# Prologue of a Fourier-mixing and MoE kernel: zero matmuls at the start, moved S1 and S2 groups, filter copies as DMAs, a split first load

## Chip, cores, metric

One core of one Trainium2 chip. The metric is the time of one launch in microseconds; a run's time is its profiled span plus about 1.8 us. Times are medians of 4 to 11 runs. Ratios come from fast runs of the same job, and are not quite the ratio of the medians quoted beside them; the brackets after them are 95% intervals.

## The reference

```python
X = np.fft.rfft(x, axis=1)                    # x: (8, 3008, 256)
Y = X * (filt_r + 1j * filt_i)[None, :, :]    # filters: (1505, 256)
y = np.fft.irfft(Y, n=3008, axis=1)
h = y.reshape(24064, 256) @ w_in              # (256, 2048)
g = np.maximum(0.01 * h, h)
out = g @ w_out                               # (2048, 256)
```

## The kernel before

The transform over 3008 = 94 x 32 points is done as matmuls: S1 (over 94), a VectorE transpose T1, S2 (over 32), a multiply with the filters, SA, a second transpose T2, SB. Then come the two MoE matmuls. For batch 0 this is the prologue, done in two halves of 128 columns (`hf`) called half 0 and half 1, or first and second half, so that work can start before all of x is there; for later batches it is woven into the MoE. The filters (`fa_sb`, `fb_sb`) are loaded into partitions 0 to 63 and copied to partitions 64 to 127 by `upper`. "On pool" groups are multiplied by GpSimd after ScalarE has copied them out of PSUM, the memory that matmuls write to (`fx`, in buffers tagged p1 and p2); the others are multiplied by VectorE.

```python
    scrp = ctx.enter_context(tc.tile_pool(name="scr", bufs=2))
    ...
    def x_load(b, n0=0, nn=N2, d0=0, dn=D):
        for lo, cnt in ((0, R1),) if b + 1 < B else ((0, 64), (64, N1 - 64)):
            nc.gpsimd.dma_start(x_sb[lo : lo + cnt, ds(n0, nn), ds(d0, dn)], ...)
    ...
    for hf in range(2):
        for n0 in (0, N2 // 2):
            x_load(0, n0, N2 // 2, hf * DH, DH)
        filt_load(fa_sb, filt_r, hf * DH, DH)
        filt_load(fb_sb, filt_i, hf * DH, DH)
    nc.gpsimd.dma_start(i1_sb[:], i1_d.ap())
    nc.gpsimd.dma_start(w_in_sb[:], moe_w_in...)
    ...
    def first_s2(hf, c, n, on_pool):
        ps = bank("ph", n, DH)
        src = paired(big[1])              # "p (e n t) -> p n e t", t = 2
        for j in range(0, n, 4):
            nc.tensor.matmul(ps[...], fwd2, src[:, ds(c + j, 4), ts(hf, DH // 2)], ...)
        ...
        if on_pool:
            xs = [scrp.tile([P, 4, DH], FP32, tag=f"p{j // 4 + 1}", ...) for j in range(0, n, 4)]
            for j, xf in enumerate(xs):
                act(xf[:], ps[:, ts(j, 4), :])
            ...                           # nc.gpsimd.tensor_tensor with fa, then fb
        else:
            ...                           # nc.vector.tensor_tensor with fa, then fb
    ...
    def upper(hf):
        for t, cp in ((fa_sb, act), (fb_sb, dve)):
            cp(t[64:P, :, ts(hf, DH)], t[0:64, :, ts(hf, DH)])
    ...
    for g in range(8):
        first_s1(0, g, two[(g // 2) % 2], (act, dve)[g % 2])
    t1_part(0, 0, True)(), t1_part(0, 1, True)()
    upper(0)
    first_s2(0, 8, 8, True)
    first_s2(0, 0, 8, False)
    first_s2(0, 20, 4, True)
    first_s2(0, 16, 4, False)
    for g in range(8):
        first_s1(1, g, two[g % 4 == 3], dve if g in (3, 5, 7) else act)
    x_load(1)
    t1_part(0, 2, True)(), t1_part(0, 3, True)()
    upper(1)
    first_sa(0, 0), first_sa(0, 16)
    first_s2(1, 8, 8, True)
    first_s2(1, 0, 8, False)
    ...                                   # cut here; the rest is in the diff below
```

## Time and profile before

| | before |
|---|---|
| time, median of 5 | 785.42 us (784.65 to 787.25) |
| TensorE busy | 97% of the span |
| second x quarter used by S1 | 12.45 us |
| first VectorE multiply of half 1 | 31.29 us |
| first MoE matmul | 45.56 us |

The prediction below shows the slices and the timeline lines that carry the argument. Timeline lines read: start, duration, engine, source line, operation, output and inputs, count, and in brackets the engine's idle time before and what ended it. Two more lines of the kernel before:

```profile
20.47 0.59 ACT L268 COPY fx_h_c<-ph 128x512 f32<-128x512 f32 x1 [0.68 <-PE ph L260]
31.29 1.23 DVE L276 TENSOR_TENSOR fy_h_c<-ph,fa_sb 128x1024 f16<-128x1024 f32 x1 [1.04 <-ACT fx_h_c L268]
```

ScalarE's copy for the third GpSimd group waits for its matmul, and VectorE's first half-1 multiply for ScalarE's copy of the S2 output. The profiled run took 787.67 us, more than any of the five timed ones. The "granted clock" below is the share of TensorE's full clock that the profile says the throttle allowed.

### The profile page before, as it was taken

How to read it: one execution, taken by the hardware profiler on the slowest of the kernel's cores; microseconds unless marked ns; L12 is line 12 of the kernel's file. 1: busy time of each engine (PE TensorE's matmuls, PEld its weight loads, DVE VectorE, ACT ScalarE, POOL GpSimd, SP SyncE). 2: the span in 40 equal slices, each digit the busy share in tenths (PEclk: the TensorE clock that was granted, in tenths of full speed). 3: DMA queues.
4: the chain of work that ended last, by engine and by line, in shares of the span. 5: the costliest groups of instructions: out<-in, count | busy, mean ns of one | idle time of the engine just before them, and what ended most of it. 6: DMA issues, size and time to landing. Idle time of an engine off the chain costs nothing.

```text
span 785.9 us, 13623 instructions
## 1 busy us (share of the span) xinstructions
PE 763.0 (97%) x5812; PEld 528.6 (67%) x5812; DVE 365.1 (46%) x459; ACT 557.0 (71%) x794; POOL 150.7 (19%) x122
## 2 busy tenths in 40 slices
PE   2799999999999999999999999999999999999998
PEld 1356677666776677866777667776677667676666
DVE  3869760784327652387316754078432765200000
ACT  3686768676687767877687775967668776666664
POOL 5773400240003400052001410024000340000000
PEclk9999999999999999999999999999999999999999
DMA  9943010501032010501014101050100101101111
GB/s 174 214 59 94 28 42 28 122 28 41 28 79 70 28 41 28 119 31 41 28 41 108 41 28 41 28 120 28 42 28 28 41 28 42 41 28 41 41 41 54
DMA packets 42013, 43.39 MB, mean 55 GB/s; under 512 B 14274, under 2 KB 40514, under 8 KB 41282
## 3 DMA queue, kind: packets, MB, share of 16 engines
q0 software_dynamic: 15760, 16.99, 13.2%
q1 hardware_dynamic: 26192, 25.53, 9.3%
q8 instruction: 45, 0.74, 0.4%
q14 instruction: 16, 0.13, 0.1%
HBM read 34.10 MB, written 24.64 MB: 75 GB/s over the span
## 4 chain that ended last, share of the span: by engine, by line
PE 93%; ACT 2%; issue 1%; DVE 0%; ACTq 0%; DVEq 0%
PE po_ps L379 41%; PE ph L365 40%; PE pf L170 3%; PE pf L237 2%; PE pf L210 2%; PE pf L225 2%; PE pf L379 1%; ACT big L181 1%; ACT gt_c L370 1%; PE pf L284 1%; PE ph L260 0%; PE ph L301 0%; DVE fy_h_c L276 0%; PE po_ps L313 0%; PE pf L301 0%
## 5 line engine op out<-in xcount | busy, mean ns | idle before, releaser
L370 ACT ACTIVATE gt_c<-ph 128x1024 f16<-128x1024 f32 x376 | 384.8, 1024 | 194.8 <-PE ph L365 193.8
L365 PE MATMUL ph<-yt,w_in_sb 128*128 128x512 f16 (+7 forms) x1728 | 386.6, 351 | 0.4 <-ACT yt L304 0.2
L379 PE MATMUL po_ps<-w_out_sb,gt_c 128*128 128x256 f16 x2944 | 381.5, 272 | 0.6 <-ACT ost_c_t L386 0.6
L379 PEld LDWEIGHTS <-gt_c 128*128 128x128 f16 x3008 | 290.7, 98 | 86.7 <-issue 1.7
L365 PEld LDWEIGHTS <-w_in_sb 128*128 128x128 f16 x1728 | 163.0, 98 | 95.2 <-issue 1.0
L218 POOL TENSOR_TENSOR y_b_g<-p_b_g,p_b_g 128x512 f16<-128x512 f32 x84 | 106.9, 1273 | 225.5 <-DVE p_b_g L216 225.5
L181 ACT CAST big<-pf 128x512 f16<-128x512 f32 x195 | 111.8, 606 | 11.8 <-PE pf L251 11.7
L193 DVE STREAM_TRANSPOSE big<-big 128x1024 f32<-128x1024 f32 x32 | 55.8, 1846 | 127.1 <-ACT big L181 126.7
L240 DVE CAST yt<-pf 128x376 f16<-128x376 f32 x112 | 56.3, 545 | 85.9 <-PE pf L237 85.9
L214 DVE TENSOR_TENSOR p_b_g<-pf,fa_sb 128x512 f32<-128x512 f32 x84 | 58.1, 692 | 38.0 <-PE pf L210 35.5
L386 ACT COPY ost_c_t<-po_ps 128x256 f32<-128x256 f32 x184 | 69.4, 377 | 6.7 <-PE po_ps L379 5.6
L201 DVE STREAM_TRANSPOSE big<-big 128x1024 f32<-128x1024 f32 x28 | 51.1, 1936 | 34.5 <-ACT big L181 34.5
L215 DVE TENSOR_TENSOR p_b_g<-pf,fb_sb 64x512 f32<-64x512 f32 x84 | 58.2, 693 | 1.1
L216 DVE TENSOR_TENSOR p_b_g<-pf,fb_sb 64x512 f32<-64x512 f32 x84 | 57.4, 683 | 1.1
L132 POOL DMA_DIRECT2D x_sb<-in_x_dram x12 | 8.5, 713 | 256.6 <-PE pf L170 255.5
L237 PEld LDWEIGHTS <-big 128*128 128x128 f16 x448 | 25.7, 98 | 13.2
L170 PE MATMUL pf<-x_sb,f_sb 94*128 94x256 f16 x224 | 33.8, 272 | 0.1
L210 PE MATMUL pf<-big,small_sb 128*128 128x512 f16 x84 | 31.8, 379 | 0.0
L225 PE MATMUL pf<-y_b_g,small_sb 128*128 128x512 f16 x84 | 31.8, 379 | 0.0
L237 PE MATMUL pf<-i_sb,big 128*128 128x94 f16 x448 | 28.7, 206 | 0.0
L170 PEld LDWEIGHTS <-f_sb 94*128 94x128 f16 x224 | 21.0, 97 | 9.5 <-issue 1.3
L347 POOL TENSOR_SCALAR fb_sb<-fb_sb 64x6144 f16<-64x6144 f16 x1 | 15.7, 15742 | 0.4 <-DVE fy_h_c L276 0.4
(45 smaller groups left out, 142.8 us busy)
## 6 DMA issues: line engine op xcount, KB each, us to landing
out_dram<-ost_c_t SPq DMA_DIRECT2D x92, 256.0 KB, 2.1
x_sb<-in_x_dram POOLq DMA_DIRECT2D x6, 1536.0 KB, 11.3
x_sb<-in_x_dram POOLq DMA_DIRECT2D x4, 384.0 KB, 11.0
w_in_sb<-in_moe_w_in_dram POOLq DMA_DIRECT2D x1, 1024.0 KB, 14.9
w_out_sb<-in_moe_w_out_dram POOLq DMA_DIRECT2D x1, 1024.0 KB, 10.2
x_sb<-in_x_dram POOLq DMA_DIRECT2D x1, 1024.0 KB, 9.1
f_sb<-fwd_const SPq DMA_DIRECT2D x4, 192.0 KB, 3.2
fa_sb<-in_filt_r_dram POOLq DMA_DIRECT2D x4, 192.0 KB, 9.8
```

What stands on the lines that cost most here:

```text
L170: nc.tensor.matmul(ps[:, j, :], f1_sb[:N1, n2, :], x_sb[:N1, n2, :], start=True, stop=True)
L181: copy(paired(dst)[:, ds(n0, nn), ds(e0, de)], ps.rearrange("p n (e t) -> p n e t", t=2))
L214: nc.vector.tensor_tensor(p1[:], ps, fa, AL.mult)
L215: nc.vector.tensor_tensor(p2[0:64], ps[64:P], fb[64:P], AL.mult)
L216: nc.vector.tensor_tensor(p2[64:P], ps[0:64], fb[0:64], AL.mult)
L218: nc.gpsimd.tensor_tensor(y1[:], p1[:], p2[:], AL.add)
L237: nc.tensor.matmul(ps[:, j, :], src[:, dt, n2, :], i1_sb[:, n2, :], start=True, stop=True)
L240: copy(yv[:, :, ds(4 * h, 4)], ps.rearrange("p c a -> p a c"))
L365: nc.tensor.matmul(ph[:, j, ds(o, ln)], w_in_sb[:, dt, ts(ct, P)], yts[b % 2][:, dt, ds(lo, ln)], start=(dt == 0), stop=(dt == NDT - 1),)
L370: nc.scalar.activation(gts[ci][:, ds(2 * g, 2), :], ph, AF.Lrelu)
L379: nc.tensor.matmul(po, gts[ci][:, ct, ts(tj, P)], w_out_sb[:, ct, :], start=(ct == 0), stop=(ct == NCT - 1))
L386: nc.scalar.copy(ost[:, tj % 2, :], po)
```

## The change

The intent: warm the TensorE clock while x is on its way, fill TensorE's wait for a PSUM buffer with S1 groups of the second half, take the second half's filter copies off ScalarE and VectorE, let VectorE's last multiplies run on, and start the first x load with a smaller piece. The diff is cut at "..."; it also moves a memset of `big[2]` behind that of the zero tile.

```diff
-    def x_load(b, n0=0, nn=N2, d0=0, dn=D):
+    def x_load(b, n0=0, nn=N2, d0=0, dn=D, parts=None):
...
-            x_load(0, n0, N2 // 2, hf * DH, DH)
+            x_load(0, n0, N2 // 2, hf * DH, DH, None if hf else ((0, 64), (64, 32)))
...
     def upper(hf):
-        for t, cp in ((fa_sb, act), (fb_sb, dve)):
+        for t, cp in ((fa_sb, nc.sync.dma_start if hf else act), (fb_sb, nc.sync.dma_start if hf else dve)):
...
+    idle = scrp.tile([P, CH], FP16, tag="p1", name="idle")
+    nc.vector.memset(idle[:], 0.0)
+    keep_warm(24)          # now 128x128 by 128x512 matmuls of the idle tile into po_ps
...
     first_s2(0, 20, 4, True)
-    first_s2(0, 16, 4, False)
+    upper(1)
     for g in range(8):
+        if g == 3:
+            first_s2(0, 16, 4, False)
         first_s1(1, g, two[g % 4 == 3], dve if g in (3, 5, 7) else act)
     x_load(1)
     t1_part(0, 2, True)(), t1_part(0, 3, True)()
-    upper(1)
     first_sa(0, 0), first_sa(0, 16)
     first_s2(1, 8, 8, True)
     first_s2(1, 0, 8, False)
     nc.gpsimd.dma_start(w_out_sb[:], moe_w_out.rearrange("(ct p) d -> p ct d", p=P))
+    first_s2(1, 16, 8, False)
     first_sa(0, 8), first_sa(0, 20)
-    first_s2(1, 16, 8, False)
     first_sa(1, 0)
...
-    keep_warm(3)
     for g in range(8, 16):
```

More of the change, by code (lines that the diff above doesn't have):

```diff
@@ L127 @@
     DH = D // 2
-    def x_load(b, n0=0, nn=N2, d0=0, dn=D):
-        for lo, cnt in ((0, R1),) if b + 1 < B else ((0, 64), (64, N1 - 64)):
+    def x_load(b, n0=0, nn=N2, d0=0, dn=D, parts=None):
+        if b + 1 < B:
+            parts = parts or ((0, R1),)
+        for lo, cnt in parts or ((0, 64), (64, N1 - 64)):
             nc.gpsimd.dma_start(
@@ L160 @@
     nc.scalar.activation(one[:], one[:], AF.Lrelu)
-    nc.vector.memset(big[2][:].rearrange("p (e n t) -> p e n t", n=Q, t=2)[:, :, NC:Q, :], 0.0)
     def s1_group(b, g, copy=nc.scalar.copy):
@@ L312, in keep_warm @@
         for _ in range(n):
-            nc.tensor.matmul(po_ps.rearrange("p a d -> p (a d)"), small_sb[:, 0, :],
-                             i1_sb[:].rearrange("p a d -> p (a d)")[:, 0:512],
+            nc.tensor.matmul(po_ps[:].rearrange("p a d -> p (a d)"), idle[:, 0:P], idle[:],
                              start=True, stop=True)
+    idle = scrp.tile([P, CH], FP16, tag="p1", name="idle")
+    nc.vector.memset(idle[:], 0.0)
+    keep_warm(24)
+    nc.vector.memset(big[2][:].rearrange("p (e n t) -> p e n t", n=Q, t=2)[:, :, NC:Q, :], 0.0)
     for g in range(8):
```

## The prediction

> **What bounds the kernel now.** I read the page first: engine shares, slices, chain, groups. Then I read the first 60 us in time order, engine by engine, because every edited line is there.
>
> ```profile
> PE 763.0 (97%) x5812; PEld 528.6 (67%) x5812; DVE 365.1 (46%) x459; ACT 557.0 (71%) x794; POOL 150.7 (19%) x122
> ...
> PE   2799999999999999999999999999999999999998
> ```
>
> TensorE is busy for 97% of the span; of 40 slices (19.6 us each) only the first two are not full. From about 46 us on, the MoE matmuls set the pace, and the diff touches none of them. So the whole effect is how much earlier the first MoE matmul can start. Split in stretches, TensorE is busy 54.0 of the 54.4 us from 45.6 to 100 us, and 499.45 of the 500 us from 200 to 700 us: a microsecond won before the MoE should reach the end nearly undiminished, and nothing more can be won.
>
> ```profile
> 9.59 1.01 PE L251 MATMUL pf<-x_sb,f_sb 94*128 94x128 f16 x8 [9.59 <-DMA x_sb<-in_x_dram]
> 12.45 1.01 PE L251 MATMUL pf<-x_sb,f_sb 94*128 94x128 f16 x8 [0.99 <-DMA x_sb<-in_x_dram]
> 17.67 1.88 PE L260 MATMUL ph<-big,small_sb 128*128 128x512 f16 x4 [3.35 <-DVE big L193]
> 22.05 0.59 PE L260 MATMUL ph<-big,small_sb 128*128 128x512 f16 x1 [1.61 <-DVE fy_h_c L276]
> 29.31 1.88 PE L260 MATMUL ph<-big,small_sb 128*128 128x512 f16 x4 [1.33 <-DVE big L193]
> 45.56 1.28 PE L365 MATMUL ph<-yt,w_in_sb 128*128 128x512 f16 x4 [0.17 <-ACT yt L304]
> ```
>
> These timeline lines (start, duration, idle before) show TensorE waiting: for the first x quarter until 9.59 us, for the second until 12.45, for the first half's transposes until 17.67, for a PSUM buffer until 22.05, for the second half's transposes until 29.31. MoE starts at 45.56. The prologue is a relay of DMA, TensorE, ScalarE/VectorE evictions and VectorE transposes, bound by no engine's throughput.
>
> ```profile
> 26.29 2.75 ACT L308 COPY fa_sb<-fa_sb 64x3072 f16<-64x3072 f16 x1
> 26.88 2.37 DVE L193 STREAM_TRANSPOSE big<-big 128x1024 f32<-128x1024 f32 x2
> 29.29 0.96 DVE L308 COPY fb_sb<-fb_sb 64x3072 f16<-64x3072 f16 x1
> 34.70 1.22 DVE L276 TENSOR_TENSOR fy_h_c<-ph,fa_sb 128x1024 f16<-128x1024 f32 x1 [1.06 <-PE ph L260]
> 36.97 2.36 DVE L292 STREAM_TRANSPOSE big<-big 128x1024 f32<-128x1024 f32 x2
> 39.69 2.37 DVE L292 STREAM_TRANSPOSE big<-big 128x1024 f32<-128x1024 f32 x2 [0.35 <-ACT big L285]
> ```
>
> The reader is to see the two filter copies that become DMAs, the 1.06 us that VectorE waits for the last S2 group, and the last transposes.
>
> **What the Trainium skill says.** (1) "TensorE: Matmul & The Clock Gate", Part 1: the array starts at half clock and is released after about 3.4 us of activity in a free-running window. The trace agrees in kind: 128x512 S2 matmuls at 29.3 to 34 us last about 600 to 630 ns and start 0.43 us apart; from 34.4 us on the same shape lasts 376 to 390 ns. The granted-clock column reads 0.50 from 31 to 34 us and 1.00 afterwards, but also 1.00 before 29 us, where durations are slow; early on I trust durations. (2) The same page puts the return to half clock after about 3.4 us of idleness. The trace doesn't fit: at 27.6 us matmuls last 379 ns, TensorE then idles 1.33 us, and at 29.31 they last 600 again. I take warmth to survive about a microsecond, not three. (3) "DMA: Bandwidth & Descriptors", Rules for kernel authors: two transfers to disjoint partition parts share the same 16 engines and gain nothing. So splitting one load into 64 and 32 rows can gain only by an earlier start. The trace shows the software queue slow at first: 20 packets from 2 to 4 us, 496 from 4 to 6, then 1201, and a steady 1433 per 2 us.
>
> **The change part by part.**
>
> *24 zero matmuls at the start.* They need only a small memset, so they start near 1.2 us. Cold spacing is 0.43 us; half that, 0.216, follows from the five warm-keeping matmuls before (1.24 us for five, the last one's latency included). In this trace the array warmed 5.1 us after work resumed at 22.05 (27.2) and 4.7 after 29.31 (34.0). So I take about 5 us cold, 12 matmuls, then 12 at 0.216 = 2.6 us: the end is near 8.8 us, before x at 9.59. Cost on the path: none. Gain: S1's 128x128 matmuls run warm. Cold, a group of four takes 0.43 us (evictions start at 13.07, 13.58, 13.93, 14.36 and end at 15.05). Warm, TensorE outruns the evictions, two engines at 0.59 and 0.69 us: first group ready 0.45 us after the second x quarter, VectorE's first 0.3 later, two of 0.69 behind it: 12.45+0.45+0.3+1.38 = 14.58, against 15.05, **0.47 us**. The gap between the x quarters (about 1.6 us if warm) may lose the clock again; I count 0.3. The 3.3 us transpose wait at 14.3 to 17.7 almost surely loses it, so S2 stays cold.
>
> *The x load split.* The first part needs fewer descriptors built before it can start, but issues cost 0.6 to 1.1 us each on GpSimd and engines are saturated from 7 us on. I count **0.2**.
>
> *S1 groups 0 to 2 ahead of the (0,16) S2 group.* Now TensorE stands 1.61 us before 22.05 with all second-half S1 behind it. Afterwards three groups (12 x 0.107 = 1.3 us) fill that hole; their x landed by about 18.3 us (issued 6.26, some 12 us to land). The buffer still comes free at 22.00, so VectorE's multiplies still run 22.68 to 23.96. Groups 3, 5, 7 are then ready in time, and VectorE follows on without gaps: 23.96 + 3 x 0.65 = 25.9, against 26.78 before. Transposes start at 25.95 instead of 26.88: **0.93 us**.
>
> *upper(1) as two DMAs.* This takes 2.75 us from ScalarE and 0.96 from VectorE. VectorE's copy lay beside TensorE's S2 (VectorE waited 1.04 us after it): worth nothing. ScalarE's made the SA evictions wait until 29.06, but those are needed only by the transposes of 36.97. The DMAs (1536 pieces per tensor, at most 717 packets per us when alone, about half when shared) start after the filters land, 22 and 24.7 us, and should land near 28 and 30.2, needed near 30 and 31.2. Hidden.
>
> *S2 (1,16) ahead of SA.* Measure from the start of second-half S2 (29.31 before). VectorE starts its last multiplies at +5.39 (34.70) before; afterwards the S2 group waits only for ScalarE's copies (+2.3), is done by +3.4, and VectorE runs on from +4.35: first T2 at +6.8 instead of +7.66. But SA moves behind S2: nine ScalarE evictions of 0.55 us queue between +4.5 and about +10, so the last T2 pair starts near +10.0 instead of +10.38. Of 0.9 us on VectorE, **0.35** remains.
>
> *keep_warm(3) removed.* It took 0.75 us, 42.31 to 43.06. But ScalarE evicts all of SB groups 0 to 7, until 43.39, idles 0.16, then takes four more. At most 0.16 plus a little: **0.2**.
>
> Sum: 0.3+0.2+0.93+0.35+0.2 = **2.0 us**. MoE starts near 43.6 instead of 45.56, and the time is 786.68-2.0 = **784.7 us**.
>
> **Rivals.** *A: the clock stays warm through the waits.* Then each half's first four S2 take 1.1 instead of 1.98 us ahead of VectorE: 2 x 0.9 us more, 782.9. For: the page's 3.4 us; against: the 1.33 us gap above. *B: TensorE gains nothing that evictions don't hold back.* If x doesn't land earlier, S1 cools between the quarters, and nine SA evictions swallow the S2 reorder, only 0.93 is left: 785.7. For: ScalarE's four SB evictions of 0.47 us and the VectorE chain, which no edit shortens. *C: the filter-copy DMAs land late.* DMA engines were over 90% busy from 5 to 23 us and share w_in from there. Two microseconds late would make VectorE and GpSimd wait at the second multiply and eat the gain: 786.7. *D: the zero matmuls overrun.* If the clock releases only after 8 us, the 24 end near 9.8, 0.2 us after x; only if it never releases do they end at 11.5 and delay S1 by 1.9, giving 786.6 without the S1 gain.
>
> **Range and chances.** The sum is 2.0 with errors of about 1 either way: B and C pull up to +1 to +2, A down to -1.8. The three runs before spread over 2.5 us, so the median adds about 1. Range **782.5 to 786.6**. Two per cent is 15.7 us; the entire wait for the first x is 9.6. A win over 2% is next to impossible, and a loss would need a wait that appears nowhere: 0.01 faster, 0.98 same, 0.01 slower.
>
> **What would show each step right or wrong.** In the changed profile: zero matmuls from about 1.2 to 9 us, starts first 0.43 then 0.216 us apart; S1 at 9.4 or so with evictions closer than 0.43; last first-half eviction near 14.6; S2 matmuls still near 600 ns after the transpose wait; second-half transposes at about 25.4 (0.93 plus 0.5 earlier); no filter copy on ScalarE there, and no VectorE wait on a filter DMA; last multiplies without the 1.06 us hole; last T2 pair at about 37.9; first MoE matmul near 43.6. S2 at 380 ns would show A; a DMA named ahead of multiplies C; zero matmuls still running when x lands D. A shift of the MoE start that the end doesn't show would break the premise that TensorE carries it through.

## The result

The changed kernel takes **796.71 us** (796.09 to 797.2, 5 runs) against 785.42 us: ratio 1.014, 95% interval 1.0123 to 1.0156. It is slower by some 11 us, far outside the predicted range, though still within 2%. These timeline lines of the changed kernel answer to those that the prediction shows:

```profile
1.23 8.07 PE L313 MATMUL po_ps<-idle 128*128 128x512 f16 x24 [1.23 <-DVE idle L317]
10.08 0.61 PE L251 MATMUL pf<-x_sb,f_sb 94*128 94x128 f16 x8 [0.78 <-DMA x_sb<-in_x_dram]
12.30 0.61 PE L251 MATMUL pf<-x_sb,f_sb 94*128 94x128 f16 x8 [1.17 <-DMA x_sb<-in_x_dram]
16.93 1.88 PE L260 MATMUL ph<-big,small_sb 128*128 128x512 f16 x4 [3.58 <-DVE big L193]
21.32 0.59 PE L260 MATMUL ph<-big,small_sb 128*128 128x512 f16 x1 [0.54 <-DVE fy_h_c L276]
22.08 0.58 ACT L268 COPY fx_h_c<-ph 128x512 f32<-128x512 f32 x1 [3.01 <-POOL fy_h_c L271]
23.14 0.70 SPq L308 DMA_DIRECT2D fa_sb<-fa_sb  x1
25.53 11.30 SPq L308 DMA_DIRECT2D fb_sb<-fb_sb  x1
26.04 2.37 DVE L193 STREAM_TRANSPOSE big<-big 128x1024 f32<-128x1024 f32 x2
28.46 1.88 PE L260 MATMUL ph<-big,small_sb 128*128 128x512 f16 x4 [0.89 <-DVE big L193]
41.39 1.23 DVE L276 TENSOR_TENSOR fy_h_c<-ph,fa_sb 128x1024 f16<-128x1024 f32 x1 [12.98 <-DMA fa_sb<-fa_sb]
54.95 1.29 PE L369 MATMUL ph<-yt,w_in_sb 128*128 128x512 f16 x4 [0.16 <-ACT yt L304]
```

S2 of half 1 starts at 28.46 instead of 29.31 us. Then VectorE stands 12.98 us before its multiply, until the copy DMA issued at 23.14 us has landed at about 41.3. GpSimd waits for the same DMA. The chain of waits of the changed kernel, in order of time (start, duration, what), shows it on the path:

```profile
23.14 18.13 DMA fa_sb<-fa_sb
41.27 0.03 issue
41.29 0.05 DVEq L276
41.34 0.04 issue
41.39 0.95 DVE fy_h_c L276
```

What the DMA engines did meanwhile is in the DMA view of the changed kernel, first from 31 to 37 us, then from 37 to 41 us. Columns: packets, MB, share of the engines (it adds up the packets' times and can pass 100%); q0 is the queue that GpSimd issues to, q1 that of the sync engine.

```profile
q0 software_dynamic: 79, 1.25, 97.7%
q1 hardware_dynamic: 80, 0.02, 2.6%
```

```profile
q1 hardware_dynamic: 2736, 0.69, 88.3%
q0 software_dynamic: 21, 0.08, 9.8%
```

From 31 to 37 us, q0 carries the load of x for batch 1 in packets of 1.25 MB / 79 = 16 KB, and q1 the copy in packets of 256 B. **They take turns packet by packet**: 79 against 80. So the copy gets 13 packets per us. When the load is done, it gets 2736 in 4 us.

Runs differ in when x lands (S1 uses the second x quarter between 10.65 and 12.45 us in the profiles), so I compare stretches of the prologue, from that moment on, in us (differences of start times in the profiles; the two kernels on the right are explained below):

| stretch, ending at the start of | before | changed | engine_copies | own_idle |
|---|---|---|---|---|
| first-half T1 transposes | 2.70 | 2.12 | 2.11 | 2.11 |
| second-half T1 transposes | 11.73 | 11.62 | 11.64 | 10.71 |
| first VectorE multiply of half 1 | 4.41 | 15.35 | 4.40 | 4.40 |
| last T2 pair | 8.40 | 7.88 | 7.25 | 7.87 |
| first MoE matmul | 5.87 | 5.68 | 5.50 | 5.53 |
| sum | 33.11 | 42.65 | 30.90 | 30.62 |

The span less the start of MoE is 740.3 us before (785.9 - 45.56), 740.2 in the changed kernel and 740.3 in the other two: a shift of the MoE start reaches the end undiminished, as the prediction assumed. The two profiled runs differ by 9.3 us (796.94 and 787.67), as the sums do (9.5); the medians differ by 11.3, since the profiled run before is 2.2 us above its own median.

### The profile page after: what moved, and what is told of

It is laid out like the page before. It is cut to its first block, busy times and chain, and to the rows that moved or that the text cites. A ratio compares the mean times of both kernels' runs of the same rounds, so it can differ in the third digit from the quotient of the medians.

```text
span 795.1 us, 13674 instructions
## 1 busy us (share of the span) xinstructions
PE 771.4 (97%) x5833; PEld 529.6 (67%) x5833; DVE 364.1 (46%) x459; ACT 554.2 (70%) x793; POOL 151.9 (19%) x124
## 4 chain that ended last, share of the span: by engine, by line
PE 91%; DMA 5%; ACT 2%; issue 1%; DVE 1%; POOL 0%; DVEq 0%; ACTq 0%; SPq 0%; POOLq 0%
PE po_ps L383 40%; PE ph L369 40%; PE pf L170 2%; PE pf L237 2%; PE pf L225 2%; DMA fa_sb<-fa_sb 2%; PE pf L210 2%; DMA fa_sb<-in_filt_r_dram 1%; DMA x_sb<-in_x_dram 1%; PE pf L383 1%; ACT big L181 1%; ACT gt_c L374 1%; DVE fy_h_c L276 0%; PE pf L284 0%; PE ph L301 0%
## 5 line engine op out<-in xcount | busy, mean ns | idle before, releaser
L284 PE MATMUL pf<-fy_h_c,small_sb 128*128 128x512 f16 x24 | 10.2, 583 | 9.3 <-DVE fy_h_c L276 9.3
```

## The experiments

Twelve kernels ran, in four jobs, each on another chip; each job timed the kernel before anew, and a comparison across jobs is told as such. Theory: the copy DMA, starved by larger packets, is the whole loss, and the rest of the change gains about 2 us. Rivals: another part costs; or the copy is slow in itself; or its bytes, not its packets, count.

### engine_copies: only the copies put back on ScalarE and VectorE

```diff
-        for t, cp in ((fa_sb, nc.sync.dma_start if hf else act), (fb_sb, nc.sync.dma_start if hf else dve)):
+        for t, cp in ((fa_sb, act), (fb_sb, dve)):
...
-    upper(1)                       # before the S1 loop
...
     t1_part(0, 2, True)(), t1_part(0, 3, True)()
+    upper(1)
```

> The changed kernel with only the second-half filter copies put back on ScalarE and VectorE, where they stood before. My theory: the whole loss is the wait of VectorE and GpSimd for the copy DMA (12.98 us of idle before the multiply at 41.39), and the rest of the change works roughly as predicted; then the multiply starts near 30.5 us, MoE near 44 us, and the time is 783.5 to 785 us, about 0.1 to 0.3% under the kernel before. Rival: another part (zero matmuls, moved groups, buffer of the idle tile) costs several us by itself; then it stays above 787 us.

Measured: 784.23 us against 786.06, ratio 0.9981 (0.9964 to 0.9998). VectorE's multiply starts 4.40 us after the transposes, as before; MoE starts at 41.69 us, earlier than I wrote, since x landed early in this profile:

```profile
28.94 1.23 DVE L276 TENSOR_TENSOR fy_h_c<-ph,fa_sb 128x1024 f16<-128x1024 f32 x1 [1.04 <-ACT fx_h_c L268]
```

The DMA copies are the whole loss; the rest of the change gains a little.

### before_dma: only the copies as DMAs, on the kernel before

```diff
-        for t, cp in ((fa_sb, act), (fb_sb, dve)):
+        for t, cp in ((fa_sb, nc.sync.dma_start if hf else act), (fb_sb, nc.sync.dma_start if hf else dve)):
...
     first_s2(0, 16, 4, False)
+    upper(1)
...
-    upper(1)                       # after the second-half T1
```

> The kernel before with one edit alone: the second-half filter copies as DMAs from the sync queue, issued where the change issues them. Theory: this alone makes the whole loss; the first copy lands near 41 us in a profile like that of before, VectorE waits some 10 us at its multiply (31.29 before), and the time is 9 to 12 us above the kernel before (795 to 798 us). Rival (the loss needs the earlier S1 and x load of the change as well): under 3 us.

Measured: 798.09 us against 785.52, ratio 1.0162 (1.0148 to 1.0176), just above what was expected. The multiply starts at 41.22 us:

```profile
41.22 1.23 DVE L276 TENSOR_TENSOR fy_h_c<-ph,fa_sb 128x1024 f16<-128x1024 f32 x1 [13.02 <-DMA fa_sb<-fa_sb]
```

The edit alone makes the loss: 12.6 us by the medians on the kernel before, and 12.5 on the changed one (796.71 against engine_copies' 784.23, of different jobs).

### late_x: the load of x for batch 1 after the multiplies

```diff
-    x_load(1)                      # after the S1 loop
...
     first_s2(1, 0, 8, False)
+    x_load(1)
     nc.gpsimd.dma_start(w_out_sb[:], ...)
```

> The changed kernel with the load of x for batch 1 issued after GpSimd's second-half multiplies instead of before the copies have landed. Theory (packet-by-packet sharing: each 256 B packet of the copy waits for one of 16 KB of that load): without the load the 2850 or so packets left at 30.5 us move at about 950 per us, so the first copy lands near 32 us instead of 41.3, VectorE's wait shrinks from 13 to about 4 us, and the time is 787 to 789 us, or a little more if x then lands too late for batch 1. Rival (the copy is slow in itself, or its issue on the sync queue is, 11.3 us for the second): the first copy still takes 15 us or more and the time stays above 794 us.

Measured: 790.5 us, ratio 1.0058 (1.0043 to 1.0073). VectorE's wait falls from 12.98 to 6.81 us; the multiply starts at 33.70 us, 1.7 us later than expected, and the time is above the expected range:

```profile
33.70 1.23 DVE L276 TENSOR_TENSOR fy_h_c<-ph,fa_sb 128x1024 f16<-128x1024 f32 x1 [6.81 <-DMA fa_sb<-fa_sb]
```

The load makes about half of the wait. Packets were as expected (some 50 per us beside w_in until 29.5 us, then 800 to 940), but the copy's first packet moves only after 25 us, though it was issued at 21.6; and the first tensor lands when almost all of both tensors have moved (some 2860 of 3072 pieces by 33 us).

### late_both: w_in moved too

```diff
-    nc.gpsimd.dma_start(w_in_sb[:], ...)    # among the first loads
...
     first_s2(1, 0, 8, False)
+    nc.gpsimd.dma_start(w_in_sb[:], ...)
+    x_load(1)                      # here as in late_x
     nc.gpsimd.dma_start(w_out_sb[:], ...)
```

> As late_x, but the load of w_in is moved behind the second-half multiplies too, so that nothing large stands in the software queue while the copies run. If sharing with w_in is the rest of the delay, the first copy lands by 28.5 us and VectorE's wait of 6.81 us (late_x) falls below 1 us. If the copy is slow in itself (4 us from issue to its first packet, then 3 us of packets), it still lands at 29 to 31 us and VectorE waits 1 to 3 us. The time is not the point, since w_in and x come late: MoE and batch 1 wait for them and it may well be above 790 us.

Measured: 791.79 us, ratio 1.0078 (1.0057 to 1.0099). VectorE no longer waits for the DMA at all:

```profile
28.80 1.23 DVE L275 TENSOR_TENSOR fy_h_c<-ph,fa_sb 128x1024 f16<-128x1024 f32 x1 [1.97 <-PE ph L259]
```

With nothing large beside it, the same copy is hidden, so it isn't slow in itself, nor is its issue. MoE starts at 41.94 us, as in engine_copies; the time is lost later, where TensorE waits 6.0 us for the late x of batch 1.

### small_x: the same load in small packets

```diff
-    x_load(1)
+    x_load(1, d0=0, dn=DH), x_load(1, d0=DH, dn=DH)
```

> The changed kernel with the load of x for batch 1 issued at the same place, but as two column halves, so that it arrives in 6144 pieces of 256 B instead of some 190 of 16 KB; bytes and time of issue are unchanged. Packet-by-packet sharing: the copy then gets every second of about 720 packets per us instead of 13 per us, so the first copy lands near 34 to 36 us instead of 41.3, VectorE waits 5 to 7 us instead of 13, and the time is 788 to 791 us. Rival (what counts is the bytes that the load takes from the engines): the first copy lands at 40 us or later and the time stays above 794 us.

Measured: 795.3 us, ratio 1.0119 (1.01 to 1.0139). The mechanism was right and the time missed. The DMA view of this kernel from 31 to 37 us has equal packets again, now of 256 B on both queues:

```profile
q0 software_dynamic: 1999, 0.51, 83.2%
q1 hardware_dynamic: 1990, 0.51, 64.1%
```

Against the 80 packets of the changed kernel the copy moves 1990 in the same six microseconds, and the first tensor is there at 35.6 us. But I had forgotten the second tensor behind it in the queue:

```profile
35.67 1.23 DVE L276 TENSOR_TENSOR fy_h_c<-ph,fa_sb 128x1024 f16<-128x1024 f32 x1 [8.06 <-DMA fa_sb<-fa_sb]
40.29 1.23 DVE L276 TENSOR_TENSOR fy_h_c<-ph,fb_sb 128x1024 f16<-128x1024 f32 x1 [3.38 <-DMA fb_sb<-fb_sb]
```

VectorE waits 8.06 us for the first copy and then 3.38 us for the second, which the changed kernel, with both landing between 41 and 42.3 us, doesn't. The neighbour's packet size, at equal bytes and nearly the same time of issue, sets the copy's rate; smaller packets for the neighbour are no cure.

### whole_rows: few large packets for the copy

```diff
-            cp(t[64:P, :, ts(hf, DH)], t[0:64, :, ts(hf, DH)])
+            if hf:                 # called after the S1 loop
+                cp(t[64:P], t[0:64])
+            else:
+                cp(t[64:P, :, ts(hf, DH)], t[0:64, :, ts(hf, DH)])
```

> The changed kernel with the copy DMA moving whole rows, both halves (twice the bytes, but 64 pieces of 12 KB per tensor instead of 1536 of 256 B), issued after the last S1 group. Packet sharing: few packets wait few turns, the first copy takes some 4 to 6 us from its issue near 24.5, so it lands by 29 to 31 us and the second by 31 to 33; VectorE's wait nearly gone, time 783.5 to 786. Rival (bytes or the DMA route are what costs): twice the bytes take as long or longer, time above 795 us.

Measured: 792.28 us, ratio 1.0081 (1.0066 to 1.0096). Twice the bytes land earlier, at 33.1 us for the first tensor and 37.7 us for the second:

```profile
33.18 1.22 DVE L276 TENSOR_TENSOR fy_h_c<-ph,fa_sb 128x1024 f16<-128x1024 f32 x1 [5.73 <-DMA fa_sb<-fa_sb]
37.79 1.23 DVE L276 TENSOR_TENSOR fy_h_c<-ph,fb_sb 128x1024 f16<-128x1024 f32 x1 [3.38 <-DMA fb_sb<-fb_sb]
```

So bytes aren't what starves the small copy; but they do cost: both queues move about 15 packets per us, and 1.6 MB at 0.2 MB per us take 8 us. My size was wrong by a factor of two.

### vector_copies: both copies on VectorE

```diff
-        for t, cp in ((fa_sb, act), (fb_sb, dve)):
+        for t, cp in ((fa_sb, dve if hf else act), (fb_sb, dve)):     # against engine_copies
```

> As engine_copies, but both second-half filter copies on VectorE (two of 0.96 us, in the stretch in which VectorE waits for S2 anyway, instead of 2.75 us on ScalarE). If ScalarE's copy holds SA evictions or the GpSimd chain back, 0.3 to 1 us faster than engine_copies; if it lies beside the transposes, equal to it within 0.3 us.

Measured: 784.53 us, ratio 0.9983 (0.9968 to 0.9998), not to be told from engine_copies at 784.23 in the same rounds. The copies were off the path where they stood; moving them wins nothing.

### own_idle: the zero tile in a buffer of its own

```diff
-    idle = scrp.tile([P, CH], FP16, tag="p1", name="idle")
+    idle = scrp.tile([P, CH], FP16, tag="idle", bufs=1, name="idle")  # against engine_copies
```

> engine_copies with the zero tile in a buffer of its own instead of one of the two p1 buffers. Theory: the idle tile holds a p1 buffer until its last use, so ScalarE's copy of S2 (0,20) waits 3.01 us for GpSimd; without that it starts some 2.2 us earlier, S1 groups 5 and 7 no longer wait, the second-half transposes start 0.6 to 0.9 us earlier, and the time falls by 0.5 to 1 us (near 783.5). Rival: the evictions had slack; same time within 0.3 us.

Measured: 783.5 us against 785.52, ratio 0.9977 (0.9964 to 0.9989). ScalarE's third copy no longer waits for GpSimd:

```profile
19.09 0.59 ACT L268 COPY fx_h_c<-ph 128x512 f32<-128x512 f32 x1 [0.68 <-PE ph L260]
```

In the changed kernel it waited 3.01 us, because the zero tile kept one of the two p1 buffers until its last use. The second-half transposes start 10.71 us after the first ones instead of 11.64. But 0.62 us of this is given back before the last T2 pair (7.87 against 7.25): in this profile the granted clock is 0.50 from 27 to 33 us, in that of engine_copies 1.00, and the SA matmuls go with it. The fall of 0.5 to 1 us that I expected is not resolved: the two ratios, of different jobs, can't be told apart.

### no_zero_matmuls and one_x_load

```diff
-    keep_warm(24)                                       # no_zero_matmuls, against engine_copies
```

```diff
-            x_load(0, n0, N2 // 2, hf * DH, DH, None if hf else ((0, 64), (64, 32)))
+            x_load(0, n0, N2 // 2, hf * DH, DH)         # one_x_load, against engine_copies
```

> engine_copies without the 24 zero matmuls at the start. Theory: S1 of the first half runs at 311 ns instead of 217 ns a matmul, the last first-half eviction ends about 0.5 us later after the second x quarter (2.6 instead of 2.0 us), and the time rises by 0.3 to 0.6 us (to about 784.7). Rival: the clock makes nothing, or the zero matmuls overrun the first x and cost: same or up to 0.3 us faster.

> engine_copies with the first x quarters loaded as one DMA of 96 rows each, as before. Theory (the 16 engines are shared, the split only changes issue order): the second x quarter lands within 0.3 us of the split one and the time is the same within 0.4 us. If the split really starts the data earlier, this run is 0.2 to 0.5 us slower.

Measured: 784.37 us for both, ratios 0.9988 (0.9974 to 1.0001) and 0.9993 (0.9981 to 1.0006). The lines of S1 groups, without and with the zero matmuls (engine_copies), end in busy us, mean ns and idle time before:

```profile
L251 PE MATMUL ph<-x_sb,f_sb 94*128 94x128 f16 x16 | 2.1, 312 | 0.0
```

```profile
L251 PE MATMUL ph<-x_sb,f_sb 94*128 94x128 f16 x16 | 1.2, 219 | 0.0
```

Without the zero matmuls S1 takes 306 to 312 ns a matmul instead of 219, and the first stretch of the table is 2.70 us instead of 2.11, a gain of **0.59 us** for the zero matmuls in the trace; the times don't resolve it. Nor does every run have it: in two of the eleven profiles with zero matmuls (vector_copies, fill_waits) the clock fell between the x quarters and the first stretch is 2.56 us, a gain of 0.14. In three (engine_copies, late_both, contiguous_s2) S1 follows the zero matmuls without a wait, so they still ran when x landed; that cost nothing, since TensorE then waited 0.78 us or more for the second quarter. The second x quarter is used at 11.14 us without the split and at 10.79, 11.65 and 12.30 us with it (engine_copies, own_idle, changed): what the split does is smaller than the scatter and stays open.

### fill_waits: zero matmuls in the waits for the transposes

```diff
+    keep_warm(12)                                       # against own_idle
     first_s2(0, 8, 8, True)
...
+    keep_warm(7)
     first_s2(1, 8, 8, True)
```

> own_idle plus 12 zero matmuls ahead of first-half S2 and 7 ahead of second-half S2, in TensorE's waits for the transposes (3.58 and 2.05 us). Theory: the clock is kept through the waits, S2 runs at 379 instead of 600 ns, VectorE's multiplies start 0.8 us earlier in each half, and the time falls by 1.2 to 2.2 us against own_idle (near 781.7). Rival: the clock is lost all the same or the fillers overrun the transposes; then the same or up to 2 us slower.

Measured: 783.83 us, ratio 0.9975 (0.9957 to 0.9993), no gain over own_idle. The fillers brought the clock back (0.50 from 12 us, 1.00 from 15), and S2 didn't care. The windows view of this kernel gives window, length, TensorE busy time and count, granted clock, DMA share and GB/s:

```profile
15.00:16.00 1.00, 1.00 (x6) 1.00 1.83 183
16.02:17.90 1.88, 1.88 (x5) 1.00 1.83 182
26.65:28.53 1.88, 1.88 (x5) 1.00 1.07 216
```

Groups of TensorE in a window from 27.0 to 27.4 us and, for the zero matmuls, from 25.0 to 26.6 us (the last numbers of interest: busy us, mean ns):

```profile
L260 PE MATMUL ph<-big,small_sb 128*128 128x512 f16 x2 | 1.0, 598 | 0.0
```

```profile
L313 PE MATMUL po_ps<-idle 128*128 128x512 f16 x7 | 1.7, 379 | 0.0
```

The zero matmuls run at 379 ns right up to S2, at a granted clock of 1.00, and S2 of the same shape takes 598 ns. In every profile with that operand, the first four S2 matmuls of each half take 1.88 us, at a granted clock of 0.50 (changed, 16.93 us) and of 1.00 (fill_waits) alike. So S2's slowness is not the clock.

### contiguous_s2: S2's operand in one block (wrong result)

```diff
-                             src[:, ds(c + j, 4), ts(hf, DH // 2)], start=True, stop=True)
+                             big[1][:, ds(hf * Q * DH + (c + j) * DH, 4 * DH)], ...)   # against fill_waits
```

> fill_waits with the moving operand of the prologue's S2 matmuls read as one contiguous block of the same half of the same buffer instead of in pairs of 2-byte elements 128 bytes apart (wrong result on purpose; waits, sizes and counts unchanged). Theory: S2's 600 ns and 0.43 us from start to start were the operand's reading, not the clock; now four take about 1.05 us at full clock instead of 1.88, VectorE's first multiply starts about 0.8 us earlier in each half, and the time is 1 to 1.8 us below fill_waits (near 782.3). Rival (S2 was at half clock after all): still 1.88 us for four and the same time.

Measured: 781.27 us against 785.78, ratio 0.9943 (0.9928 to 0.9957); the output is wrong.

```profile
14.55 1.03 PE L260 MATMUL ph<-big,small_sb 128*128 128x512 f16 x4
```

Four S2 matmuls take 1.03 instead of 1.88 us, and the gain is larger than expected. It was how the operand is read: in pairs of 2-byte elements, 128 bytes from pair to pair. (The edit takes away the distance and a dimension of the access pattern together.) The Trainium skill, "SBUF — State Buffer", Door 1, says that SBUF is read in lines of 16 bytes, that each access which crosses to a new line pays a penalty, and that a line needs at least two hits to be read at full rate. The penalty for new lines fits; the two hits don't: this operand has two elements in a line and is still slow (598 ns against 379). The run bounds what a better layout could win, some 2.5 us by the two medians (783.83 and 781.27, of different jobs). In the profiles MoE starts 2.7 us earlier counted from the second x quarter (27.84 against 30.50), but 0.45 of that lies in the first stretch, before S2, where fill_waits' S1 ran at half clock: about 2.2 us are S2's. It is not a usable kernel, since the transposes would have to write that layout.

**The best correct version** is own_idle, with 0.9977 of the kernel before, its interval clear of 1, so about 0.2% faster, and faster than the changed kernel by some 13 us (across jobs). engine_copies, vector_copies and fill_waits (0.9975) can't be told from it.

## Why the prediction was wrong

**The step that failed** is "*upper(1) as two DMAs*". It gave the copies "at most 717 packets per us when alone, about half when shared", and concluded "Hidden". Sharing halves turns, not rates: the copy got one packet for every packet of its neighbour, that is about 48 per us beside w_in and 13 beside x, not 350. The rate that I had read (717) was that of a queue full of 256 B packets; I did not look up how large the packets were in the stretch in which the copies would run, though the kernel before shows it, here from 26 to 27 us, when w_in moves in packets of 4 KB:

```profile
q0 software_dynamic: 60, 0.24, 118.9%
```

The copies were to land near 28 and 30.2 us; they landed at 41.3 and 42.2. The Trainium skill tells of this turn-taking on a page that the prediction cites, "DMA: Bandwidth & Descriptors", Queues, rings and completion order: each engine goes round robin between the queues that have work, a packet at a time. I read only that the engines are shared. Rival C named the right wait and allowed it two microseconds; it measures 15.35 - 4.41 = 10.94 us in the table. So the sentence that a loss "would need a wait that appears nowhere" was at odds with my own rival C. The 0.98 for "same" came true only because 2% is 15.7 us, not by the reasoning.

**The clock reading** in "What the Trainium skill says", point 2, failed too: "TensorE then idles 1.33 us, and at 29.31 they last 600 again. I take warmth to survive about a microsecond". S2 lasts some 600 ns at either clock (fill_waits, contiguous_s2). The granted-clock column, which I set aside there, fits: it falls only after 30 us, and SA's matmuls from 31 us on start 0.43 us apart. Earlier I was right to distrust it: it reads 1.00 while S1 takes 312 ns in no_zero_matmuls, and while the first zero matmuls of the changed kernel start 0.43 us apart. That reading made rival A worthless from the start: a warm clock wins nothing in S2 (0 instead of 1.8 us).

**The other steps**, each by the table:
- *24 zero matmuls.* End foreseen 8.8 us, measured 9.3 (7.9 to 9.3 over the profiles); worked out 0.47 us, counted 0.3, measured 0.58 (2.70 to 2.12), confirmed by taking them out. The clock held across both x quarters in that profile, not in all: 0.14 us in two of eleven.
- *S1 groups 0 to 2 ahead.* Foreseen 0.93 us. The changed kernel gained 0.11, since the zero tile took a buffer from ScalarE's copies; this wait I had not seen in the diff. With a buffer of its own it is 1.02 us (0.95 in fill_waits, at another clock). The mechanism was right, its condition overlooked.
- *S2 (1,16) ahead of SA.* Foreseen 0.35 us; measured 1.15 (engine_copies, granted clock 1.00 there) and 0.53 (own_idle, clock 0.50). The queue of nine evictions is shorter when SA runs at full clock.
- *keep_warm(3) removed.* Foreseen 0.2 us; measured 0.37 and 0.34 in these two kernels.
- *The split.* Foreseen 0.2 us; open.
- *A slip in a rival's sum.* Rival D's 786.6 leaves out the 0.3 us of S1 gain that it gives up: 784.7 + 1.9 + 0.3 = 786.9.

Without the copies and the split the sum foreseen was 1.8 us; engine_copies shows 33.11 - 30.90 = 2.2 us and own_idle 2.5 us in the profiles. Their times against before are 1.8 and 2.0 us lower. So the prediction was right, within the scatter, about the sum of all but one part and the split, though single parts missed both ways, and the part that failed was five times as large as the rest together (10.94 against 2.2 us). Its range also failed there: with rival C allowed no more than two microseconds, a time beyond 787 us had no place in it.

## What to carry to other kernels

Before moving a copy to a DMA queue, look at the packet sizes of what will be in flight beside it: a transfer of many small packets gets one turn per neighbour's packet, so beside 16 KB packets 256 B pieces nearly stand still (13 per us here). Keeping such a copy clear of large loads hid it in late_both, but no run here made the DMA copies pay; ScalarE and VectorE did them off the path. Before calling a matmul cold, hold its duration against another of the same shape at the same granted clock; the operand's layout may be what is slow. A helper tile that lives long must not share a rotating buffer tag with tiles on the path.

## What the Trainium skill lacked or had wrong

- "DMA: Bandwidth & Descriptors", Queues, rings and completion order: it gives the turn-taking, confirmed here (79 against 80, 1999 against 1990 packets), but not what follows for a queue of small packets: 13 packets of 256 B per us beside 16 KB packets, 48 beside those of w_in (4 KB), about 330 beside others of 256 B, 680 to 940 nearly alone. Its packet of several descriptors isn't seen in these counts.
- The same page, Rules for kernel authors: large transfers are advised; that they hold back small ones of another queue (an 18.1 us landing, hidden when no large one is near) is not said there.
- The same page, Specifications, gives about 0.6 us to the first byte for transfers issued by the sync engine. These traces show 3 to 4 us from the issue of the copy to its first packet, with other loads in flight on the other queue; the cause stays open.
- "TensorE: Matmul & The Clock Gate", Part 1: it puts the return to half clock after some 3.4 us of idleness, though its passage on PSUM-queue cycling knows short idles that make the clock swing. In fill_waits S1 ran at full rate until 9.75 us, TensorE stood for 1.13 us (and for 0.64 us before S1), and from 11 to 12 us the granted clock was 0.53; in nine other profiles with zero matmuls gaps of 0.8 to 1.2 us at the same place left S1 at full rate.
- The same page gives matmul durations by size and clock alone; here the moving operand's layout takes a 128x512 matmul from 379 to 598 ns at a granted clock of 1.00. "SBUF — State Buffer" gives the lines, but its two hits per line were not enough here.
